# Backward chain of a memory-augmented attention kernel: gradient stores from the last step of a block on, two loads and one gather moved with them

## The chip, the cores and the metric

The kernel runs on one core of one Trainium2 chip. The metric is the device time of one execution in microseconds (us), and the time of a kernel is the median of its runs. Before the change it is 2886.74 us, the median of three runs between 2880.99 and 2886.81 us.

## What is computed

The reference is the forward pass and all gradients of `x + A(layernorm(x)) + B(layernorm(x))`. B is a two-layer network with a squared ReLU. A is a recurrent attention: the 2048 rows are cut into 64 segments of 32 rows, and each segment attends to itself and to 8 memory rows that the segment before it produced.

```python
for s in range(n_seg):                       # 64 segments of 32 rows
    h = concat([mem, xs], axis=1)            # 8 memory rows + 32 rows
    q, k, v = h @ Wq, h @ Wk, h @ Wv         # 512 -> 32 heads of 128
    p = softmax(where(mask, q @ k.T * scale, -1e9))
    o = (p @ v) @ Wo
    mem = o[:, :M]                           # carried to the next segment
    outs.append(o[:, M:])
```

The gradients run through the segments in the reverse order, because the gradient of `mem` is carried from segment s to segment s - 1. That part is the backward chain.

## The kernel before

Activations and weights are bf16, sums are float32 in PSUM. The kernel has stages that follow each other: the norm and network B, the forward chain, a stage for the memory rows of all blocks at once (line 992 on), the backward chain (lines 1158 to 1498), and the products that make the weight gradients (line 1501 on).

The backward chain takes one step for each of the 64 segments. Four steps make a block, so there are 16 blocks. The text numbers steps 0 to 3 in the order in which they run within a block, and blocks 0 to 15 in the order in which they run; the program's own index `b` counts down, and the last block that runs is the one with `b == 0`. A step computes the gradient of the attention output (`o0mm`, `o1mm`, line 374), turns it (`o0fl`, `o1fl`), forms the score gradients (`s0`, `d10` to `d40`, which write the tile `gS`), and from them the gradients of value, key and query: TensorE makes them in the PSUM tiles `b_pp` (`vp`, `kp`, `qp`, lines 1389, 1391 and 623), and ACT or DVE evict them (`vea`, `kea0`, `qeb1` and so on) into three tiles `gv`, `gk`, `gq` (the dictionary `G4`, line 1189). These hold the gradients of all four steps of a block in one buffer each, of 8 KB a partition. From them the gathers `vg`, `kg`, `qg` (line 492) sum the gradient of the input into `ps_gR`, and `ra` to `Hb` close the chain to the next step.

The order of all work is written out by hand. `B_ORDER` (line 1158) has one string for each of the four steps, and `play` (line 652) goes through the names: each name is a small function that emits instructions. A plain name is an operation of a step; with "L." ahead it belongs to a block. The number of plus signs says by how much the operation is ahead of its place. `L.x++` in the string of step 3 belongs to the block whose step 3 runs, `L.x+` to the block before. The engines take their own instructions in this order, each waiting on semaphores only for what it needs. An engine whose next instruction has nothing to wait for runs ahead of the others, so a name's place in the string fixes the order on its engine, not a moment.

The names that the change touches:

- `vo0`, `vo1`, `ko0`, `ko1`, `qo0`, `qo1` (line 1243): the six stores of a block's `gv`, `gk`, `gq` to the DRAM tensor `S_GB`, 512 KB each, issued on the SP queue. A value store covers half of the groups; a key or query store covers half of the heads of each group. The next block's evictions overwrite the same tiles, so they wait for the stores.
- `ldk0`, `ldk1` (line 1342): two loads of 128 KB on the SP queue into `b_kNL`, the key rows of the memory positions. They are read by `qp0` and `qp1` (line 623). The tile has one buffer, so they wait for the last `qp` of the block before.
- `L.G0` (line 1256): the first eight of the matmuls that gather the gradient of the memory rows ("left" rows) of a block into `ps_RL`. It reads `b_gvL`, which `vla` writes. In step 3 it stands after `tu1`.

Names that stay but stand around them on the SP queue: `vtr` (line 1346, a transposing load into `b_vl` for a coming step), `L.ldt` (line 632, a transposing load), `L.qtr` (line 1279, a transposing DMA from `b_gqL` to `gNat`), `L.lq` (line 1221, the load into `b_gqL` for the next gathers), `L.qst` (line 1288, a store of `gNat`), `L.sx` (line 1291, a store of `b_XT`). The GpSimd queue (POOL) carries the other loads: `ldp`, `ldq`, `ldn` for each step (`b_P`, `b_qN`, `b_kN`, lines 1332, 1339, 1340) and `L.ldv`, `L.ldk` for each block (lines 1305 to 1310). `pb` (line 1337) copies `b_P` on POOL.

Of the kernel before, what the change touches and what calls it, by code (L numbers as in the profile page):

```python
# [26 lines left out]
def kernel(  # L27
# [35 lines left out]
    L = M + SEG  # L63
# [146 lines left out]
    with sb("p1b", 2) as p1b, sb("p1", 1) as p1:  # L210
# [90 lines left out]
        for rb in range(NRB):  # L301
# [38 lines left out]
            xb = xq[rb]  # L340
# [307 lines left out]
    def on_engines(act, vec):  # L648

        return dict([(n, acp) for n in act.split()] + [(n, vcp) for n in vec.split()])  # L650
# [50 lines left out]
    with psum("fr", 4) as fr, psum("fpp", 1) as fpp, \  # L701
# [259 lines left out]
        with tc.manual_schedule():  # L961
            steps, lefts = [], {-1: left_projections(1, {})}
            for s in range(NSEG):
                steps.append(fwd(s))
            for b in range(NB):
                lefts[b] = left(b)
            steps[0]["ld0"]()
            for p in range(2):
                for g in range(HG):
                    x = slice(g * KH + 4 * p, g * KH + 4 * p + 4)  # L970
                    dma(Wo[:, x], A_Wo.rearrange("h e d -> e h d")[:, x])

            early = []
            after = {"ob0": 2, "ob1": 2, "L.S1": 2, "L.ex0": 2, "L.ex1": 2, "L.tu1": 4, "L.ob1": 2, "L.G1": 1, "L.G0": 1}
            after_o = {"L.ra": 6, "L.tb": 5, "L.xt": 5}

            def done(k):
                if k == "L.lq":  # L980
                    early.append(xlp.tile([P, KH, HG, NL], BF16, name="l_vT0", tag="XL1"))
                    turned_rows(early[0][:], SEQ[0], 2)
                for q, m in ((TURNS, after.get(k, 0)), (TURNS_O, after_o.get(k, 0))):
                    for i in range(m):
                        ps = fr.tile([P, 8 * P], BF16, name="ps_wt", tag="r")
                        turn_weight(ps, *q.pop(0), acp if k in ("L.S1", "L.ex0", "L.ex1") else (acp, vcp)[i % 2])
            for n in range(-1, NB + 4):
                play(F_ORDER, n, steps, lefts, lambda s: s, lambda b: b, done)
# [5 lines left out]
    with sb("la", 2) as la, sb("ls", 2) as ls, sb("lo", 1) as lo_, sb("wg", 2) as wg, psum("lpp", 1) as lpp, psum("lr", 4) as lr:  # L994
# [161 lines left out]


    B_ORDER = (
# [17 lines left out]
        "ta++++ rb++++ Ha++++ tb++++ Hb++++",  # L1176
# [5 lines left out]
        "ta++++ L.qst+ kla1++++ tb++++ L.H0++ Ha++++ Hb++++")  # L1182
    ENGS = on_engines(
        "L.ra0 kea0 keb0 keb1 kla0 kla1 o0ev o1ev qea0 qea1 qeb0 ra vea veb vla vlb",
        "kea1 klb0 klb1 o0te o1te qeb1")
    with sb("bq", 1) as bq, sb("bt", 1) as bt, sb("bs", 2) as bs, sb("be", 1) as be, psum("bpp", 1) as bpp, psum("br", 4) as br:
# [30 lines left out]
        def left(b):  # L1217
            B_ = block(b)
            ps, st, o = {}, {}, {}
# [19 lines left out]
            for t, n in enumerate("qkv"):  # L1239
                for x in range(2):  # L1240
                    def so(n=n, t=t, gs=slice(2 * x, 2 * x + 2) if n == "v" else slice(0, HG),
                           ks=slice(0, KH) if n == "v" else HALF[x]):
                        dma(S_GB[b, t][:, gs, ks], G4[n][:, gs, ks].rearrange("p g k j r -> p g k (j r)"))
                    o["%so%d" % (n, x)] = so

            jobs = [(turned_heads(Wqkv[t]), src[n], k) for t, n in ((2, "v"), (1, "k"), (0, "q")) for k in range(KH)]
            for i in range(4):
# [213 lines left out]
        with tc.manual_schedule():  # L1461
# [3 lines left out]
            for b in range(NB):  # L1465
                lefts[b] = left(b)
# [35 lines left out]
    with sb("p5a", 1) as p5a, sb("p5h", 1) as p5h, sb("p5", 2) as p5, sb("p5g", 1) as p5g, \  # L1502
# [118 lines left out]
        for i, (t, g) in enumerate(COLS):  # L1621
# [14 lines left out]
            for x, js in enumerate(jobs[k:k + each] for k in range(0, len(jobs), each)):  # L1636
                if x in ((), (), (2, 6), (2, 6))[i] if i < 4 else x == 4:
                    b = todo.pop(0)
# [48 lines left out]
```

## Time and profile before

| | |
|---|---|
| Median of three runs | 2886.74 us |
| The profiled execution's own time | 2877.56 us |
| Its span (first to last instruction) | 2875.8 us |
| Mean granted TensorE clock | 0.976 of full speed |
| TensorE matmuls busy | 2677.1 us (93% of the span) |
| Backward chain, first step's start to last step's end | about 1336 to 2290 us |

The profile is of one execution. Times in it count from the start of the span. A row of the windows view gives a stretch, its length, the busy time of each engine in it with the number of instructions in brackets, the granted TensorE clock, the busy share of the 16 DMA engines and the rate in GB/s. A row of the waits view says who waited for whom, how long in total, how often, and the longest wait. In a timeline row the last bracket is the idle time of the engine just before, and what ended it; "issue" stands there when the profile shows nothing that the engine waited for.

### The profile page before, as it was taken

What the parts mean: (1) busy time and instruction counts of PE and PEld (TensorE: products, weight loads), DVE (VectorE), ACT (ScalarE), POOL (GpSimd) and SP (SyncE); (2) the same over time, 40 slices, a digit from 0 to 9 for tenths busy, and PEclk for the clock granted to TensorE, in tenths of its full rate; (3) what the DMA queues carried; (4) which work ended last, traced back from release to release, by engine and by line L of the source; (5) the groups of instructions that cost most, each with busy time, mean ns of one, the idle gap of its engine ahead of it and who ended that gap; (6) DMA issues with size and microseconds to landing.
All of it is one profiled execution on the core that took longest, in us unless ns stands there. A gap on an engine that the chain in (4) does not pass through costs nothing.

```text
span 2875.8 us, 116940 instructions
## 1 busy us (share of the span) xinstructions
PE 2677.1 (93%) x52315; PEld 1444.3 (50%) x52405; DVE 1277.7 (44%) x3755; ACT 1001.4 (35%) x2330; POOL 664.9 (23%) x1289
## 2 busy tenths in 40 slices
PE   7998999999999996988988999989998899999999
PEld 3444555555555555465544455545454444444444
DVE  4534656666666654444444455544454401100000
ACT  2324444444444545232433333333333311111111
POOL 1010000000000001223433333433334334322221
PEclk9999999999999998999999999999999999999999
DMA  9765589899899998996677766886787799999992
GB/s 254 262 207 170 157 203 222 206 218 222 206 215 225 207 219 204 286 243 181 163 171 210 182 172 176 182 219 167 173 179 186 223 271 246 212 211 212 218 218 65
DMA packets 839066, 586.77 MB, mean 204 GB/s; under 512 B 638001, under 2 KB 727618, under 8 KB 835234
## 3 DMA queue, kind: packets, MB, share of 16 engines
q1 hardware_dynamic: 796034, 450.52, 69.3%
q0 software_dynamic: 42384, 128.63, 14.9%
q8 instruction: 411, 6.73, 1.0%
q14 instruction: 93, 0.76, 0.1%
q10 hardware_dynamic: 144, 0.13, 0.0%
HBM read 184.95 MB, written 248.79 MB: 151 GB/s over the span
## 4 chain that ended last, share of the span: by engine, by line
PE 82%; DMA 6%; issue 4%; DVE 4%; SPq 2%; ACT 1%; POOL 1%; ACTq 0%; DVEq 0%; POOLq 0%
PE ps_gw L1645 19%; PE ps_proj L374 15%; PE ps_gR L492 11%; PE ps_R L492 4%; PE ps_tr L167 3%; PE ps_L L374 3%; PE b_pp L623 3%; DMA b_qN<-S_A 2%; PE ps_RL L1256 2%; PE f_pp L623 2%; PE ps_sc L464 2%; PE ps_h L310 2%; PE ps_B L345 2%; PE ps_gxb L354 2%; PE f_T L528 2%
## 5 line engine op out<-in xcount | busy, mean ns | idle before, releaser
L1645 PE MATMUL ps_gw<-gn,HNc 128*128 128x512 bf16 x1884 | 414.6, 379 | 1.9
L1645 PEld LDWEIGHTS <-HNc 128*128 128x128 bf16 x1920 | 187.9, 98 | 223.8
L419 ACT CAST f_N<-ps_proj 128x512 bf16<-128x512 f32 x320 | 184.0, 581 | 195.5 <-PE ps_proj L374 185.7
L1579 ACT CAST wt<-ps_gw 128x512 bf16<-128x512 f32 x128 | 73.4, 589 | 440.6 <-PE ps_gw L1645 387.1
L374 PEld LDWEIGHTS <-X 128*32 128x32 bf16 x5760 | 144.3, 96 | 137.5 <-DVE X L537 21.2
L884 POOL COPY kM<-f_kT 128x256 bf16<-128x256 bf16 x64 | 25.8, 403 | 750.0 <-DVE f_kT L422 562.6
L1562 DVE TENSOR_TENSOR gx<-ps_rows,gb 128x512 f32<-128x512 f32 x16 | 11.1, 692 | 396.9 <-PE ps_rows L1560 396.9
L492 PE MATMUL ps_gR<-Wv,gv 128*32 128x512 bf16 x2048 | 144.9, 404 | 4.9 <-issue 4.7
L492 PE MATMUL ps_gR<-Wk,gk 128*32 128x512 bf16 (+1 forms) x2048 | 140.9, 387 | 8.0 <-issue 6.0
L1645 PE MATMUL ps_gw<-GOc,gn 128*128 128x512 bf16 x626 | 139.2, 380 | 2.2 <-DMA GOc<-in_grad_out_dram 1.3
L492 PE MATMUL ps_R<-Wo,OT 128*32 128x256 bf16 x4096 | 129.3, 275 | 8.1 <-DMA Wo<-in_A_Wo_dram 3.8
L419 ACT CAST gON<-ps_proj 128x512 bf16<-128x512 f32 x128 | 75.0, 586 | 161.9 <-PE ps_proj L374 161.9
L374 PE MATMUL ps_proj<-Wo,GT 128*32 128x512 bf16 x2048 | 124.6, 384 | 6.6 <-DVE GT L1301 5.0
L492 PE MATMUL ps_gR<-Wq,gq 128*32 128x512 bf16 (+1 forms) x2048 | 126.3, 356 | 4.4 <-issue 4.4
L374 PE MATMUL ps_proj<-Wq,X 128*32 128x512 bf16 x1920 | 127.8, 380 | 1.2 <-issue 1.1
L1580 POOL DMA_DIRECT2D out_dram<-wt x120 | 65.0, 543 | 265.4 <-ACT wt L1579 239.3
L374 PE MATMUL ps_proj<-Wk,X 128*32 128x512 bf16 x1920 | 124.8, 382 | 1.7 <-issue 1.1
L419 ACT CAST gk<-b_pp 128x256 bf16<-128x256 f32 x192 | 69.2, 379 | 159.0 <-PE b_pp L623 96.6
L374 PE MATMUL ps_proj<-Wv,X 128*32 128x512 bf16 x1920 | 121.5, 378 | 0.0
L1332 POOL DMA_DIRECT2D b_P<-S_A x63 | 33.9, 537 | 370.3 <-DVE gST L482 120.1
L1337 POOL COPY PD<-b_P 32x320 bf16<-32x320 bf16 x256 | 115.5, 451 | 10.0 <-PE ps_tr L167 1.3
L492 PEld LDWEIGHTS <-OT 128*32 128x32 bf16 x4096 | 104.5, 97 | 16.5 <-issue 10.6
(291 smaller groups left out, 5276.6 us busy)
## 6 DMA issues: line engine op xcount, KB each, us to landing
S_A<-f_N SPq DMA_DIRECT2D x64, 512.0 KB
out_dram<-wt POOLq DMA_DIRECT2D x134, 128.0 KB, 5.2
S_A<-f_N SPq DMA_DIRECT2D x64, 256.0 KB
S_GB<-gv SPq DMA_DIRECT2D x32, 512.0 KB
S_GB<-gk SPq DMA_DIRECT2D x32, 512.0 KB
S_GB<-gq SPq DMA_DIRECT2D x32, 512.0 KB
b_kN<-S_A POOLq DMA_DIRECT2D x63, 256.0 KB, 4.3
b_qN<-S_A POOLq DMA_DIRECT2D x63, 256.0 KB, 4.0
```

Of the source, the lines that this page charges most:

```text
L167: nc.tensor.transpose(ps_ap, in_ap, ident[base:base + k, base:base + k])
L310: nc.tensor.matmul(ps[:], lhsT=W1[:, dc, fc * P:(fc + 1) * P], rhs=HT[:, dc, :], start=(dc == 0), stop=(dc == DC - 1))
L345: nc.tensor.matmul(psB[:], lhsT=aT[:, fc, rc * P:(rc + 1) * P], rhs=W2[:, fc, :], start=(fc == 0), stop=(fc == FC - 1))
L354: nc.tensor.matmul(psG[:], lhsT=gh1T[:, fc, rc * P:(rc + 1) * P], rhs=W1T[:, fc, :], start=(fc == 0), stop=(fc == FC - 1))
L374: nc.tensor.matmul(o, lhsT=hT[:, dc, :], rhs=x, start=(dc == 0), stop=(dc == DC - 1), tile_position=(0, 32 * g))
L419: nc.scalar.copy(out, in_)
L492: nc.tensor.matmul(R[32 * g:32 * g + 32, 0:(cs.stop - cs.start) * P].rearrange("p (a b) -> p a b", b=P), lhsT=XT(k, g), rhs=x[:, cs, :], s ...
L623: nc.tensor.matmul(o, lhsT=N_[32 * g:32 * g + m, kk * P:(kk + 1) * P], rhs=X(kk)[32 * g:32 * g + m], start=(i == 0), stop=(i == len(jobs) ...
L1337: nc.gpsimd.tensor_copy(PD[32 * g:32 * g + 32, g], C["P"][32 * g:32 * g + 32, :, KW - L:KW])
L1579: nc.scalar.copy(wt[:], ps[:])
L1580: eng(dst, wt[:])
L1645: nc.tensor.matmul(ps[:], lhsT=l(rc), rhs=r(rc), start=(n == 0), stop=(n == RC_ALL - 1))
```

## The change

All edits are in `B_ORDER` and in one line that names the stores.

```diff
     B_ORDER = (
-        "L.vo0+ o0mm++++ o1mm++++ L.vo1+ o0ev++++ pb+++ xa+++ L.xt ldk0+++ o1ev++++ o0fl++++ xb+++ L.ra0+ vp0++++ "
-        "o0te++++ L.G2+ ldk1+++ vea++++ s0++++ ...
+        "L.vo0+ o0mm++++ o1mm++++ L.vo1+ L.Qo1+ o0ev++++ pb+++ xa+++ L.xt o1ev++++ o0fl++++ xb+++ L.ra0+ vp0++++ "
+        "o0te++++ L.G2+ vea++++ s0++++ ...
...
-        "vlb++++ d40++++ d11++++ vg0++++ kp0++++ L.tb+ kla0++++ tu0++++ d21++++ qp0++++ vg1++++ d31++++ keb0++++ "
-        "d41++++ kea0++++ kg0++++ kp1++++ L.qtr+ qeb0++++ tu1++++ L.G0++ klb0++++ qp1++++ L.ldv++ L.ta+ qea0++++ "
-        "qg0++++ qeb1++++ kea1++++ keb1++++ qea1++++ kg1++++ L.lq++ klb1++++ qg1++++ L.I0++ ra++++ L.ldk++ rb++++ "
-        "ta++++ L.qst+ kla1++++ tb++++ L.H0++ Ha++++ Hb++++")
+        "vlb++++ d40++++ d11++++ vg0++++ L.G0++ kp0++++ L.Vo0++ L.Vo1++ L.tb+ kla0++++ tu0++++ d21++++ qp0++++ vg1++++ d31++++ keb0++++ "
+        "d41++++ kea0++++ kg0++++ kp1++++ L.qtr+ qeb0++++ tu1++++ klb0++++ qp1++++ L.ldv++ L.ta+ qea0++++ "
+        "qg0++++ qeb1++++ kea1++++ L.Ko0++ keb1++++ qea1++++ kg1++++ L.lq++ klb1++++ qg1++++ L.I0++ ra++++ L.ldk++ L.Ko1++ rb++++ "
+        "ta++++ L.qst+ ldk0++++ ldk1++++ L.Qo0++ kla1++++ tb++++ L.H0++ Ha++++ Hb++++")
...
-                    o["%so%d" % (n, x)] = so
+                    o["%so%d" % (n.upper() if b > 0 else n, x)] = so
```

For every block but the last, the stores have capital names and stand from step 3 of their own block on. For the last block they keep the small names and the old places. As built, the SP queue of one block boundary takes its DMAs in these orders:

```
before: vtr, ldt, qtr, lq, qst, vo0, vo1, ldk0, ldk1, ko0, qo0, qo1, sx, vtr, ko1, vtr
after:  vtr, ldt, Vo0, Vo1, qtr, Ko0, lq, Ko1, qst, ldk0, ldk1, Qo0, Qo1, sx, vtr, vtr
```

In the built program `Vo0` waits for the second eviction of `gv` in step 3 (ACT), `lq` waits for the landing of `qtr`'s transposes, whose source it overwrites, and `ldk0` waits for the last `qp1` of the block. TensorE, ACT, DVE and POOL execute the same instructions as before; on TensorE only `G0` stands elsewhere, ahead of `kp0` in step 3 of all 16 blocks.

2 rows, old and new, of the table B_ORDER are left out of this document.

## The prediction

> **What bounds the kernel now.** I began with the page: how much TensorE idles at all.
>
> ```profile
> span 2875.8 us, 116940 instructions
> PE 2677.1 (93%) x52315; PEld 1444.3 (50%) x52405; DVE 1277.7 (44%) x3755; ACT 1001.4 (35%) x2330; POOL 664.9 (23%) x1289
> q8 instruction: 411, 6.73, 1.0%
> ```
>
> TensorE is busy 93% of the span, so time is won only where it idles or runs at a lower clock. To find where, I cut the chain at the first `ps_proj` matmul of each step and asked for the windows of 15 blocks (1 to 15): all steps 1, then 2, then 3 (each the step ahead of a boundary), then 0. Of each answer this is the sum row; one quick step of either kind stands ahead of it for the last two.
>
> ```profile
> sum 196.30, PE 194.00 PEld 107.77 DVE 118.76 ACT 80.29 POOL 74.42; mean PE 12.93 PEld 7.18 DVE 7.92 ACT 5.35 POOL 4.96
> sum 196.00, PE 189.30 PEld 105.21 DVE 95.03 ACT 84.39 POOL 65.47; mean PE 12.62 PEld 7.01 DVE 6.34 ACT 5.63 POOL 4.37
> 1855.80:1869.50 13.70, 13.57 (x365) 7.48 (x368) 7.50 (x24) 5.50 (x15) 7.98 (x16) 1.00 0.81 179
> sum 227.70, PE 209.59 PEld 114.00 DVE 118.62 ACT 82.45 POOL 126.75; mean PE 13.97 PEld 7.60 DVE 7.91 ACT 5.50 POOL 8.45
> 1756.40:1770.70 14.30, 13.24 (x368) 7.33 (x360) 6.94 (x24) 6.03 (x16) 4.21 (x8) 1.00 0.82 216
> sum 273.10, PE 220.83 PEld 113.57 DVE 103.39 ACT 90.75 POOL 72.58; mean PE 14.72 PEld 7.57 DVE 6.89 ACT 6.05 POOL 4.84
> ```
>
> Steps 1 and 2 take 13.1 us and are full. Step 3 takes 227.7 / 15 = 15.2 us and step 0 takes 18.2 us, though quick ones take 13.70 and 14.30. So there is an excess of 273.1 - 15 x 14.3 = 58.6 us in the steps 0 and of 227.7 - 15 x 13.7 = 22.2 us in the steps 3. That is all this change can win. Who TensorE waits for in the chain, by the waits view:
>
> ```profile
> PE b_pp L623 <- issue: 28.3, 19, 4.7
> PE b_pp L623 <- DMA b_qN<-S_A: 15.4, 9, 5.6
> PE ps_gR L492 <- issue: 15.1, 12, 4.0
> PE b_pp L623 <- DVE gS L582: 7.2, 10, 1.0
> PE ps_gR L492 <- DVE gk L422: 1.5, 2, 1.2
> ACT gk L419 <- DMA S_GB<-gk: 15.1, 6, 3.3
> SPq L1221 <- DMA gNat<-b_gqL: 44.6, 15, 4.0
> ```
>
> The largest entries have no releaser ("issue"). I read them as code that arrives late: the page's instruction queue brings 6.73 MB in 411 packets, about 104,800 matmuls and weight loads / 411 = 255 instructions each, over the DMA engines that the stores use. The second entry is a load that lands late. So both are DMA; the DMA share around one boundary (step 3 from 1678.5, step 0 from 1693.6, step 1 from 1712.7) shows when:
>
> ```profile
> 1684.00:1687.00 3.00, 2.35 (x90) 1.45 (x94) 2.38 (x8) 1.22 (x5) 1.44 (x4) 1.00 0.43 87
> 1687.00:1690.00 3.00, 3.00 (x106) 1.54 (x102) 1.00 (x4) 0.67 (x3) 3.00 (x7) 1.00 0.76 217
> 1690.00:1699.00 9.00, 8.81 (x188) 5.08 (x178) 4.30 (x16) 4.09 (x10) 3.15 (x7) 1.00 0.99 329
> 1699.00:1702.00 3.00, 1.61 (x72) 0.85 (x73) 1.52 (x5) 0.37 (x1) 0.54 (x1) 1.00 1.08 382
> 1702.00:1707.00 5.00, 3.60 (x40) 1.22 (x39) 0.57 (x2) 1.04 (x4) 0.00 (x0) 0.57 1.10 270
> ```
>
> The engines are full from 1690 to 1707, 17 us, of which 13.4 lie in step 0. TensorE starves from 1699 on, and then its granted clock falls to 0.57.
>
> The Trainium skill (Runtime: NRT & Kernel Launch, Instruction fetch mechanics) has code arrive in blocks of 256 instructions, and the crossing into the next "mostly hidden". The block size agrees; by the hiding, the two issue rows (43.4 us) would be no DMA matter, and rival 3 below would be the likeliest. Their place in the full stretches speaks against it.
>
> **The change part by part.** First the SP queue at that boundary, as it ran before:
>
> ```profile
> 1681.27 1.47 SPq L1279 DMA_TRANSPOSE gNat<-b_gqL  x1
> 1686.59 0.33 SPq L1221 DMA_DIRECT2D b_gqL<-S_GQL  x1
> 1686.97 0.43 SPq L1288 DMA_DIRECT2D S_GL<-gNat  x1
> 1687.44 1.79 SPq L1243 DMA_DIRECT2D S_GB<-gv  x2
> 1689.33 2.36 SPq L1342 DMA_DIRECT2D b_kNL<-S_NL  x2
> 1691.79 1.25 SPq L1243 DMA_DIRECT2D S_GB<-gk  x1
> 1693.08 1.53 SPq L1243 DMA_DIRECT2D S_GB<-gq  x2
> ...
> 1701.35 1.19 SPq L1243 DMA_DIRECT2D S_GB<-gk  x1
> ```
>
> The stores named for step 0 are issued in step 3 already, because SP runs ahead. So the change moves less than its names say. *The gather.* In step 3 TensorE ends `vg0`, waits for `gS`, and then runs `kp0`; `G0` takes 0.61 us later on:
>
> ```profile
> 1684.60 0.20 PE L623 MATMUL b_pp<-gS,b_qN 32*128 32x40 bf16 x4 [0.65 <-DVE gS L582]
> 1687.99 0.61 PE L1256 MATMUL ps_RL<-Wv,b_gvL 128*32 128x512 bf16 x8
> 1683.38 0.27 ACT L419 CAST b_gvL<-b_pp 128x128 bf16<-128x128 f32 x1
> ```
>
> `G0` needs `b_gvL`, whose last eviction ends at 1683.65, before the gap opens at 1683.95. So eight matmuls of 0.61 us fill a gap of 0.65 us, and leave their old place without a wait there, since `qp1` behind them was ready. All gS waits are 7.2 us in 10 cases: the term is -7.2 us, between 0 (if code arrives late at that place) and 16 x 0.61 = -9.8.
>
> *The value stores* go ahead of `qtr`: ready at 1683.65, they start 1687.44 - 1683.65 = 3.8 us earlier, into engines with room: 3 x (1 - 0.43) + 3 x (1 - 0.76) = 2.4 us of full work. With as many bytes in all, the full stretch would end 2.4 us earlier: 11.0 instead of 13.4 us in step 0, -18%. If the step-0 excess shrinks in proportion: -58.6 x 0.18 = -10.5 us. In step 3 the full stretch grows by the same 2.4 us to what is there: 3.6 us from 1690 on and 5.5 from 1678.5 to 1684 with transposes, a quarter more; of its excess without the gS waits, 22.2 - 7.2 = 15.0, that is +4.0. Net -6.5 us. Bounds: the whole step-0 excess (-58.6) and the step-3 excess doubled (+15).
>
> *The second key store* comes from 1701.35 ahead of the query stores. The next block's key evictions wait 15.1 us for it on ACT; behind ACT stands the key gather, and TensorE's own wait for `gk` is 1.5 us. I take -1.5 (0 to -15.1).
>
> *What it costs on SP.* `lq` may start only when `qtr` has landed, 1686.59 - 1681.27 = 5.3 us after `qtr` began. Now `qtr` begins after the value stores' 1.79 us of issue, at 1685.4, so `lq` starts at 1690.7, or at 1693.6 if the 1 MB ahead holds it for 1 MB / 329-382 GB/s = 2.9 us. SP works in order: behind `lq` wait `Ko1`, `qst`, both `b_kNL` loads, both query stores, `sx` and the next `vtr`. With the issue times above (0.33 + 1.25 + 0.43, then half of 2.36) the first `b_kNL` load has been issued at 1693.9 to 1696.8 instead of 1690.5. Who waits for it is `qp0` of step 0, 7.3 us into that step in block 11, which starts at 1992.20:
>
> ```profile
> 1999.47 0.20 PE L623 MATMUL b_pp<-gST,b_kNL 32*128 32x32 bf16 x4 [0.66 <-issue]
> 1692.74 7.36 DMA b_qN<-S_A
> ```
>
> The need is at 1693.6 + 7.3 = 1700.9. No row has the landing of a `b_kNL` load. The nearest is `b_qN`'s, 7.36 us in the same crowd, twice the bytes, which makes 1701.3 to 1704.2: 0.4 to 3.3 us late. With half of that delay nothing is late. Bounds 0 and 15 x 3.3 = +50; I take +2, because the value stores ahead are gone earlier and the nine `b_qN` waits already push `qp0` back. The query stores move later too, towards the evictions that overwrite `gq`; the same stall would cover both. With POOL's loads unchanged in order, the sum is -7.2 - 6.5 - 1.5 + 2 = -13.2 us: 2877.56 - 13.2 = 2864.4 for the profiled execution. The median of the runs stands 9.18 above that execution, so 2873.5 for the median.
>
> The clock is in the excess already (clock 0.57 above follows 1.61 us busy in 3.00). The Trainium skill (TensorE: Matmul & The Clock Gate, The HAM clock gate) lowers the clock only after an idle window of some 3.4 us; here it fell after shorter waits, so the trace differs, and a short stall saved counts for more than by the page.
>
> **The rivals.** *1. The crowd thins out for good*, and step 0 comes near its floor. For it: the blocks whose value stores already began early. In four stretches (a step 3 and the step 0 behind it; the first and the last are shown, then the sum of all four) they began 4.4, 6.8, 5.6 and 5.0 us into step 3, against 1687.44 - 1678.5 = 8.9 at the boundary above:
>
> ```profile
> 1382.60:1412.60 30.00, 26.62 (x725) 14.71 (x728) 13.56 (x42) 11.53 (x31) 12.67 (x24) 1.00 0.79 228
> 1974.00:2006.50 32.50, 28.96 (x729) 15.46 (x732) 14.95 (x47) 11.53 (x31) 13.11 (x26) 0.95 0.82 225
> sum 127.20, PE 112.68 PEld 60.54 DVE 58.65 ACT 46.12 POOL 51.98; mean PE 28.17 PEld 15.14 DVE 14.66 ACT 11.53 POOL 12.99
> 1386.98 1.55 SPq L1243 DMA_DIRECT2D S_GB<-gv  x2
> 1979.03 0.96 SPq L1243 DMA_DIRECT2D S_GB<-gv  x2
> ```
>
> They take 127.2 / 4 = 31.8 us, the other eleven (500.8 - 127.2) / 11 = 34.0. Eleven times 2.2 and the gather make -31 us: 2855.7. Against it: there `qtr` had gone first, and the other stores were early too.
>
> *2. SP stalls at `lq`* (the slower side): value stores hold `qtr`, `lq` holds `b_kNL`, and `qp0` waits. It decides once the load lands over 7.3 us into step 0. Price 2 us in each of 15 boundaries, +30, less the gather's 7.2 and the key store's 1.5: +21, 2908. For it: SP waits here 3.0 us a block even now (44.6 in 15). Against it: the late `b_qN` (9 waits) already holds the matmuls ahead of `qp0`.
>
> *3. The waits only move*: what step 0 wins comes back in step 3, where code is now late among `kp` and `qp`; the gather's gain is left, and 2 us of it lost: 2881.5, at the edge of what can be told. For it: the bytes are the same, SP had run ahead anyway.
>
> **How the numbers follow.** Chances: forecast 0.35 (its own range 2865 to 2882), rival 1 0.17, rival 2 0.30, rival 3 0.18. A measurement here tells about 0.2%, 5.8 us, from no change. Faster: 0.33 + 0.17 + 0.02 = 0.52; same: 0.02 + 0.12 = 0.14; slower: 0.30 + 0.04 = 0.34. The range 2852 to 2908 leaves out half of rival 2 and a quarter of rival 1, 0.19.
>
> **What would show it.** The gather: the gS wait of 7.2 us gone from TensorE's waits. The stores: mean step 0 near 17.5 us, step 3 near 15.0, the ACT wait for `S_GB` gone. Rival 1: step 0 under 16.5. Rival 2: `lq` issued over 12 us into step 3, TensorE waiting for `b_kNL`, or ACT for the `gq` stores. Rival 3: issue waits in step 3 up by what they lose in step 0. A step 3 above 17 us would prove the forecast wrong.

## The result and the profile after

| | before | after |
|---|---|---|
| Median of 20 runs each | 2888.54 us | 2875.47 us |
| Lowest to highest run | 2864.89 to 2906.11 us | 2860.19 to 2895.03 us |
| Ratio, 95% interval | 1 | 0.9958 [0.9940, 0.9976] |
| Profiled execution | 2877.56 us | 2877.35 us |

The change is faster by 13.1 us (6.9 to 17.3 us by the interval). Here and below, the ratios leave out the few executions that are over 1.5% slower than the fastest of their kernel, and the medians in us do not. A single execution lies up to 24 us from the median, so one profile cannot show such a difference in its span:

```profile
span 2875.6 us, 116922 instructions
PE 2672.8 (93%) x52315; PEld 1447.4 (50%) x52405; DVE 1277.0 (44%) x3755; ACT 1001.7 (35%) x2330; POOL 665.8 (23%) x1289
```

The span is 0.2 us shorter than before's. The difference lies inside: the backward chain (first step's start to last step's start) takes 932.7 us instead of 939.1, but in this execution it began 11.9 us later, behind stages that the change does not touch, and what follows its last step's start took 5.7 us less. So I compare stretches of the chain. These are the windows of the same 15 blocks as in the prediction, all steps 1, then 2, 3 and 0; of each answer the sum row.

```profile
sum 196.90, PE 194.65 PEld 108.41 DVE 118.70 ACT 80.20 POOL 73.98; mean PE 12.98 PEld 7.23 DVE 7.91 ACT 5.35 POOL 4.93
sum 195.10, PE 187.71 PEld 104.45 DVE 94.94 ACT 84.41 POOL 66.32; mean PE 12.51 PEld 6.96 DVE 6.33 ACT 5.63 POOL 4.42
sum 233.00, PE 209.69 PEld 116.27 DVE 117.66 ACT 82.47 POOL 125.89; mean PE 13.98 PEld 7.75 DVE 7.84 ACT 5.50 POOL 8.39
sum 260.40, PE 217.20 PEld 113.30 DVE 103.67 ACT 90.91 POOL 73.38; mean PE 14.48 PEld 7.55 DVE 6.91 ACT 6.06 POOL 4.89
```

Steps 1 and 2 stay within 1 us of before (196.3 and 196.0). The steps 0 lose 12.7 us (from 273.1), the steps 3 take 5.3 us more (from 227.7). How far such sums can be trusted shows in the run without the exception for the last block, further down: up to its last step it has the order of the change, and its execution gave 255.3 us for the steps 0 and 227.6 us for the steps 3. So two executions of the same order lie some 5 us apart in each sum, and the loss in the steps 0 is clear, the 5.3 us in the steps 3 are not. Who waits in the chain now (the waits view; who for whom, total, times, longest):

```profile
PE b_pp L623 <- issue: 28.5, 23, 3.2
PE ps_gR L492 <- issue: 19.8, 17, 3.8
PE b_pp L623 <- DMA b_qN<-S_A: 8.5, 4, 3.8
PE b_pp L623 <- DMA b_kNL<-S_NL: 2.3, 4, 1.1
PE b_pp L623 <- DVE gS L582: 1.9, 3, 1.3
ACT gq L419 <- DMA S_GB<-gq: 4.7, 5, 1.1
SPq L1221 <- DMA gNat<-b_gqL: 61.9, 15, 5.2
```

Against before, TensorE's wait for `gS` falls from 7.2 to 1.9 us, and that for `b_qN` from 15.4 to 8.5. ACT's wait for the key stores (15.1) is gone, and one for the query stores (4.7) is there. The unnamed issue waits do not fall: 48.3 us in these two rows, 43.4 before. They change their place: summed over the 15 boundaries, all issue waits of TensorE in the steps 0 fall from 34.4 to 26.9 us, and those in the steps 3 rise from 8.9 to 19.5. SP waits longer at `lq`, 61.9 instead of 44.6 us. One boundary of after in windows (step 3 begins at 1697.1, step 0 at 1712.5, step 1 at 1728.5), and then SP's timeline there:

```profile
1703.00:1706.00 3.00, 2.97 (x112) 1.48 (x100) 1.96 (x6) 1.41 (x5) 2.22 (x5) 1.00 0.96 339
1706.00:1709.00 3.00, 2.05 (x84) 1.02 (x68) 0.98 (x3) 0.70 (x2) 2.92 (x7) 1.00 1.26 81
1709.00:1712.50 3.50, 3.48 (x66) 2.14 (x70) 0.98 (x4) 0.70 (x2) 2.19 (x5) 1.00 1.06 387
1712.50:1715.50 3.00, 3.00 (x57) 1.61 (x53) 1.63 (x7) 1.63 (x4) 0.00 (x0) 1.00 1.05 385
1715.50:1718.50 3.00, 2.96 (x108) 1.93 (x104) 2.38 (x8) 1.81 (x6) 0.00 (x0) 1.00 1.06 380
1718.50:1721.50 3.00, 1.04 (x48) 0.51 (x40) 0.67 (x3) 0.00 (x0) 0.54 (x1) 1.00 1.39 333
1721.50:1724.50 3.00, 3.00 (x80) 1.28 (x80) 1.00 (x3) 1.41 (x5) 0.53 (x1) 1.00 0.49 111
```

```profile
1701.66 1.41 SPq L1243 DMA_DIRECT2D S_GB<-gv  x2
1703.11 1.58 SPq L1279 DMA_TRANSPOSE gNat<-b_gqL  x1
1704.81 0.57 SPq L1243 DMA_DIRECT2D S_GB<-gk  x1
1710.22 0.33 SPq L1221 DMA_DIRECT2D b_gqL<-S_GQL  x1
1710.66 0.54 SPq L1243 DMA_DIRECT2D S_GB<-gk  x1
...
1713.80 1.60 SPq L1243 DMA_DIRECT2D S_GB<-gq  x2
```

The value stores go out 4.6 us into step 3 and fill the engines (0.96, 339 GB/s). Behind them the transposes of `qtr` occupy them (1.26) while few bytes move (81 GB/s). `lq` waits for those transposes and leaves 13.1 us into step 3; the second key store and the query stores stand behind it. The crowd ends at about 1721.5, 9 us into step 0, where before it ended at 1707, 13.4 us in. It costs TensorE 1.96 us of one window, and in these windows the clock stays at 1.00.

### The profile page after: what moved, and what is told of

Read it like the earlier page. It is cut to its first block, busy times and chain, and to the rows that moved or that the text cites. A ratio compares the mean times of both kernels' runs of the same rounds, so it can differ in the third digit from the quotient of the medians.

```text
span 2875.6 us, 116922 instructions
## 1 busy us (share of the span) xinstructions
PE 2672.8 (93%) x52315; PEld 1447.4 (50%) x52405; DVE 1277.0 (44%) x3755; ACT 1001.7 (35%) x2330; POOL 665.8 (23%) x1289
## 3 DMA queue, kind: packets, MB, share of 16 engines
q0 software_dynamic: 42384, 128.63, 15.2%
## 4 chain that ended last, share of the span: by engine, by line
PE 84%; DMA 6%; issue 4%; DVE 4%; ACT 1%; SPq 1%; POOL 0%; ACTq 0%; DVEq 0%; POOLq 0%
PE ps_gw L1645 19%; PE ps_proj L374 16%; PE ps_gR L492 11%; PE ps_R L492 5%; PE ps_tr L167 3%; PE ps_L L374 3%; PE b_pp L623 3%; PE ps_RL L1256 2%; PE ps_sc L464 2%; PE f_pp L623 2%; PE ps_w L1106 2%; PE ps_h L310 2%; PE ps_B L345 2%; PE ps_gxb L354 2%; PE ps_ga L317 2%
## 5 line engine op out<-in xcount | busy, mean ns | idle before, releaser
L419 ACT CAST f_N<-ps_proj 128x512 bf16<-128x512 f32 x320 | 184.0, 581 | 196.0 <-PE ps_proj L374 189.3
L492 PE MATMUL ps_R<-Wo,OT 128*32 128x256 bf16 x4096 | 131.8, 279 | 11.9 <-issue 6.3
L492 PEld LDWEIGHTS <-OT 128*32 128x32 bf16 x4096 | 105.7, 98 | 21.0 <-issue 14.1
```

The lines of the kernel that those rows point to most:

```text
L419: nc.scalar.copy(out, in_)
L492: nc.tensor.matmul(R[32 * g:32 * g + 32, 0:(cs.stop - cs.start) * P].rearrange("p (a b) -> p a b", b=P), lhsT=XT(k, g), rhs=x[:, cs, :], s ...
```

## The experiments

Every ratio is against the kernel before on the same chip. A profile is one execution: the sums over 15 steps that stand with a run belong to it alone.

**The gather alone** (the kernel before, `G0` moved):

```diff
-vg0++++ kp0++++ ... tu1++++ L.G0++ klb0++++
+vg0++++ L.G0++ kp0++++ ... tu1++++ klb0++++
```

> The kernel before with the left gather G0 alone ahead of kp0 in step 3; the stores and loads stay. Theory (the gather fills the wait for gS): TensorE's wait for gS in the chain falls from 7.2 us in 10 cases to under 2.5 us, the sum of the 15 steps 3 falls by some 5 us from 227.7, the steps 0 stay at 273 within what one execution differs from the next (15 us); time 0.995 to 1.000 of before. Rival (the whole gain of the change is in the stores): the gS wait goes, but the code that arrives late takes its place: steps 3 at 227 or above, time 1.000.

Measured: 1.0008 [0.998, 1.0037] (2889.95 us). The steps 3 take 225.4 us against 227.7 in before, the steps 0 282.2 against 273.1. The next block's key evictions wait longer for the key stores (the waits view; ACT's row was 15.1 before):

```profile
PE b_pp L623 <- DVE gS L582: 3.8, 3, 1.7
ACT gk L419 <- DMA S_GB<-gk: 26.8, 9, 4.4
DVE gk L422 <- DMA S_GB<-gk: 10.1, 4, 3.9
```

Of TensorE's 3.8 us for `gS` only 0.3 lie in a step 3, so the wait there goes away as expected, but no time is won by it that these runs can tell; the interval allows at most 5.8 us. In this execution the issue waits in the steps 3 are 14.1 us instead of 8.9.

**The stores without the gather** (the change, `G0` back behind `tu1`):

```diff
-vg0++++ L.G0++ kp0++++ ... tu1++++ klb0++++
+vg0++++ kp0++++ ... tu1++++ L.G0++ klb0++++
```

> The changed kernel with the left gather back in its old place: stores and loads moved alone. Theory: the gS wait stays near 7 us; the sum of the steps 0 falls from 273 to about 262, the sum of the steps 3 rises by 4 to 232; ACT's wait of 15.1 us for the key stores is gone; time 0.996 to 0.999 of before. Rival (the stores only move the waits): steps 0 and 3 together stay at 500.8 within 5 us and the time is 1.000. Rival (the SP queue stalls at lq and costs time): together over 510 us, TensorE waits for b_kNL over 10 us.

Measured: 0.9972 [0.9938, 1.0006] (2876.81 us), steps 3 238.9, steps 0 248.8. The wait for `gS` came to 4.1 us in 6 cases, not near 7, though `G0` stands in its old place. The ratio cannot be told from the whole change, nor quite from no change. The stores' order carries the gain as far as it can be seen; the run with the value stores alone, below, shows it more clearly.

**`qtr` ahead of the value stores** (the change, SP's old order of these two):

```diff
-kp0++++ L.Vo0++ L.Vo1++ ... kp1++++ L.qtr+ qeb0++++
+kp0++++ L.qtr+ L.Vo0++ L.Vo1++ ... kp1++++ qeb0++++
```

> The changed kernel with the transposes of b_gqL (qtr) ahead of the value stores on SP again, so that lq is not held by 1 MB of stores. Theory (lq costs SP time behind the value stores): SP's wait at lq for the transposes, 61.9 us in 15 cases in the changed kernel, falls to 45 or less; the second key store, the b_kNL loads and the query stores start 2 to 4 us earlier; TensorE's wait for b_kNL (2.3 us) and ACT's for the query stores (4.7 us) go; time 0.3% under the changed kernel, 0.992 to 0.996 of before. Rival (nothing that TensorE waits for hangs on lq): the SP order changes as said, and the time is that of the changed kernel, 0.996 of before; with the crowd packed into a shorter time the code waits in steps 3 and 0 may even grow.

Measured: 1.0004 [0.9972, 1.0036] (2884.83 us). SP's wait at `lq` is gone, and so is the gain. Steps 3 and 0, then two rows of the waits:

```profile
sum 239.40, PE 213.78 PEld 117.11 DVE 118.59 ACT 82.46 POOL 126.45; mean PE 14.25 PEld 7.81 DVE 7.91 ACT 5.50 POOL 8.43
sum 257.00, PE 217.24 PEld 113.77 DVE 102.26 ACT 90.45 POOL 70.07; mean PE 14.48 PEld 7.58 DVE 6.82 ACT 6.03 POOL 4.67
```

```profile
PE b_pp L623 <- DMA b_qN<-S_A: 16.8, 10, 4.8
SPq L1221 <- DMA gNat<-b_gqL: 6.9, 4, 4.0
```

So the wait that the prediction priced at +2 us does not cost here: without it the ratio is 0.46% higher, though the ends of the two intervals (0.9972 and 0.9976) still touch. With `lq` free, the second key store leaves on the mean 4.8 instead of 2.5 us ahead of step 0, and the two query stores 1.3 and 0.5 us ahead of it instead of 0.4 and 1.3 us behind: the stores stand closer together. `b_qN`, loaded beside them on POOL's queue, is late again, 16.8 us in all. The two sums of this execution, 496.4 us together, are hardly above the 493.4 us of the change, so the loss rests on the ratio alone.

**No stores in blocks 0 to 14** (the kernel before; the stores of these blocks are left out, and the products at the end read the stored block in their place):

```diff
-dma(S_GB[b, t][:, gs, ks], ...)
+if b == 0: dma(S_GB[b, t][:, gs, ks], ...)
...
-S_GB[4 * q + x, t][:, g]
+S_GB[0, t][:, g]
```

> The kernel before without the stores of gv, gk and gq of 15 of the 16 blocks; the weight gradients are then formed from the stored block alone, read as often, so that the stage behind the chain has the same work. Theory (the excess of steps 0 and 3 is the stores' traffic, through code and loads that arrive late): the steps 0 come to 14.3 to 15 us each (sum 215 to 225 instead of 273.1), the steps 3 to 14.2 (213 instead of 227.7), TensorE's issue waits fall from 51 us to under 10, its wait for b_qN from 15.4 to under 2; time 55 to 70 us under before, 0.976 to 0.981. Rival (code arrives late whatever the stores do, or the POOL loads make the crowd): issue waits stay over 25 us, the steps 0 over 250, and the time falls by less than 30 us.

Measured: 0.9822 [0.9772, 0.9873] (2834.02 us). Steps 3 and 0, then TensorE's waits:

```profile
sum 228.20, PE 210.21 PEld 113.95 DVE 118.55 ACT 82.46 POOL 126.97; mean PE 14.01 PEld 7.60 DVE 7.90 ACT 5.50 POOL 8.46
sum 202.40, PE 197.90 PEld 109.36 DVE 103.58 ACT 90.45 POOL 66.70; mean PE 13.19 PEld 7.29 DVE 6.91 ACT 6.03 POOL 4.45
```

```profile
PE b_pp L623 <- issue: 13.5, 15, 3.6
PE b_pp L623 <- DVE gS L582: 8.4, 12, 0.9
PE ps_gR L492 <- issue: 4.6, 6, 1.7
```

The steps 0 lose 70.7 us and come to 13.5 us each. So the floor is lower than the 14.3 us that the prediction took, and all of the excess there belongs to the stores. The steps 3 do not change (228.2 against 227.7): their excess is not the stores'. The issue waits fall from 43.4 to 18.1 us, and no wait for `b_qN` over 0.2 us is left.

**No stores, and the gather** (the kernel of the run before, `G0` moved as in the first run):

> The kernel before without the stores of gv, gk and gq of 15 blocks (the weight gradients are formed from the stored block alone) and with the left gather ahead of kp0. Theory (the gather fills a gap of 0.65 us that is real, and the crowd of the full kernel hides it): the gS wait falls from 8.4 us to under 2, the sum of the steps 3 from 228.3 by 6 to 222, the time to 2827, 0.9795 of before against 0.9822 without the gather. Rival (the gap comes back at the next wait of TensorE on DVE or ACT, or code is late instead): the gS wait goes, but the steps 3 stay at 226 to 230, and the time stays at 0.982.

Measured: 0.9753 [0.9701, 0.9805] (2814.04 us). The steps 3 fall to 216.5 us, from 228.2, and TensorE's wait for `gS` from 8.4 to 0.9:

```profile
sum 216.50, PE 204.73 PEld 115.81 DVE 118.26 ACT 82.40 POOL 127.76; mean PE 13.65 PEld 7.72 DVE 7.88 ACT 5.49 POOL 8.52
PE b_pp L623 <- DVE gS L582: 0.9, 3, 0.3
```

With no crowd, the steps 3 are 11.7 us shorter with the gather moved, of which the wait for `gS` is 7.5; the rest is no more than two executions differ by, and the two ratios overlap in their intervals. The issue waits in the steps 3 stay (8.1 without and 8.5 with the move), where beside the stores they rose from 8.9 to 14.1. So it seems that with the crowd late code takes the place of the wait that is saved; these are single executions, and it is not shown.

**The query stores later** (the change, `Qo0` behind `sx` and `Qo1` behind `vtr`, both in step 0):

```diff
-L.vo1+ L.Qo1+ o0ev++++ ... L.sx+ vg0++++ ... vtr++++ L.ko1+ ... ldk1++++ L.Qo0++ kla1++++
+L.vo1+ o0ev++++ ... L.sx+ L.Qo0+ vg0++++ ... vtr++++ L.Qo1+ L.ko1+ ... ldk1++++ kla1++++
```

> The changed kernel with the first query store behind sx and the second behind the transposing load vtr in step 0, so that the last 1 MB of stores is spread further. Theory (the gain of the change is that the stores of a block are spread out, the hold at lq included, and loads and code get through between them): TensorE's wait for b_qN falls from 8.5 us to under 5, its issue waits from 51 to about 45; the price is ACT waiting for the query stores, 4.7 us before, now up to 25 us; time 0.993 to 0.998 of before. Rival (what counts is that the stores are over early in step 0): the steps 0 rise from 260 to 270 or more, and the time is 1.000 or above.

Measured: 0.9922 [0.9887, 0.9957] (2857.43 us), the lowest ratio of all kernels that compute everything, and it beats before. Against the change (0.9940 to 0.9976) the intervals overlap, so that it also beats that one is likely, not shown. Steps 3 and 0, and the waits:

```profile
sum 232.90, PE 209.84 PEld 116.55 DVE 120.09 ACT 82.46 POOL 131.00; mean PE 13.99 PEld 7.77 DVE 8.01 ACT 5.50 POOL 8.73
sum 243.20, PE 209.84 PEld 113.72 DVE 102.65 ACT 91.11 POOL 70.96; mean PE 13.99 PEld 7.58 DVE 6.84 ACT 6.07 POOL 4.73
```

```profile
PE b_pp L623 <- DMA b_qN<-S_A: 4.3, 7, 1.2
ACT gq L419 <- DMA S_GB<-gq: 23.9, 12, 3.4
```

The steps 0 lose another 17.2 us against the change, though ACT now waits 23.9 us for the late query stores. What such a wait of ACT costs, if anything, is less than what is won.

**`qtr` first and the query stores late** (the two edits above together):

> The kernel with late query stores (ratio 0.9922) with `qtr` put back ahead of the value stores, as in the run with `qtr` first (ratio 1.0004). The wait of SP at `lq` then falls from 59.0 us to under 10 us again, but the query stores are spaced by their places in the order and not by that wait. Theory (the wait at `lq` was worth keeping only because it held the query stores back): with them held back by hand, its loss costs little, the ratio is 0.991 to 0.995, TensorE's waits for b_qN stay under 9 us and the steps 0 near 243 us. Rival (what cost the run with `qtr` first its gain is the order itself: the transposes of `qtr` lie among the value stores and slow what runs beside them in step 3): the ratio is 0.997 to 1.001, the steps 3 take over 238 us as they did there (239.1) and the b_qN waits are near 16 us.

Measured: 0.9930 [0.9898, 0.9961] (2867.11 us); the steps 3 take 230.6 and the steps 0 253.9 us.

```profile
PE b_pp L623 <- DMA b_qN<-S_A: 11.7, 9, 2.3
SPq L1221 <- DMA gNat<-b_gqL: 6.6, 3, 4.5
```

The wait at `lq` is gone here too, but with the query stores held back by hand the gain is there. Its interval and that of `qtr` first (0.9972 to 1.0036) do not meet. So `qtr` ahead of the value stores is not by itself what cost that run its gain: where the query stores stand decides it. In the change it is the wait at `lq` that holds them back, and with them the second key store and the loads of `b_kNL`, which were not tried by themselves. The `b_qN` wait and the steps 0 came out higher than the theory had them (11.7 us for under 9, 253.9 for 243), in an execution 9.4 us above its median.

**The value stores alone early** (the kernel before):

```diff
-vg0++++ kp0++++ L.tb+
+vg0++++ kp0++++ L.Vo0++ L.Vo1++ L.tb+
...
-o["%so%d" % (n, x)] = so
+o["%so%d" % (n.upper() if b > 0 and n == "v" else n, x)] = so
```

> The kernel before with the two value stores alone moved to step 3 (behind kp0); key stores, query stores, b_kNL loads and the gather stay where they were. Theory (value stores into free DMA time, and the hold at lq delaying what follows, are the gain): the steps 0 fall from 273 to 255 to 262, b_qN's wait from 15.4 to about 9, and ACT's wait for the second key store stays at 10 us or more; time 0.996 to 0.999 of before. Rival (the second key store, which no longer comes at 7 us into step 0, is the gain): steps 0 at 268 or above, time 1.000.

Measured: 0.9936 [0.9901, 0.9971] (2864.18 us), steps 3 242.9, steps 0 245.2. As far as these runs can tell, it gets as much as the whole change, so none of the other moves is shown to win anything on top. ACT waits 20.6 us for the key stores, more than the 15.1 before, and the kernel is faster all the same.

**The key store alone early** (the kernel before):

```diff
-L.ko0+ d30++++ ... vtr++++ L.ko1+ kg0++++
+L.ko0+ L.ko1+ d30++++ ... vtr++++ kg0++++
```

> The kernel before with the second key store alone moved, from behind the transposing load in step 0 to directly behind the first key store; four stores then leave in one burst. Theory (spreading is the gain): ACT's wait for the key stores (15.1 us) goes, but the burst makes code or b_qN later, steps 0 at 270 or above; time 0.999 to 1.005. Rival (the second key store's place was a part of the gain, as the prediction had it with 1.5 us): steps 0 under 268, time 0.997 or less.

Measured: 0.9988 [0.9955, 1.0021] (2888.08 us), steps 3 224.1, steps 0 277.2; ACT still waits 13.7 us for the key stores and TensorE 15.8 for `b_qN`. This part has no gain that can be told. It draws the bunch closer: the second key store leaves on the mean 1.5 us ahead of step 0, where before it left 6.4 us behind its start.

**`b_qN` loaded earlier** (the change, the load ahead of `pb` in POOL's order of step 0):

```diff
-o0ev++++ pb+++ ... ldp++++ ldq+++ veb++++
+o0ev++++ ldq+++ pb+++ ... ldp++++ veb++++
```

> The changed kernel with step 0's load of b_qN ahead of the copies of b_P and of the loads of b_kN and b_P on the POOL queue; it starts 3 us earlier. Theory (b_qN is late because it is the last of 0.6 MB of loads in a crowd): TensorE's wait for b_qN goes from 8.5 us to under 2, that for b_kN or b_kNL rises by less than 3 us, the steps 0 fall from 260 by 5 to 10; time 0.991 to 0.995 of before. Rival (code is late there anyway, so that another issue wait takes the place): the b_qN wait goes, the issue waits rise by as much, and the time stays at 0.996.

Measured: 0.9946 [0.9913, 0.9978] (2867.27 us), steps 3 237.4, steps 0 264.3. The wait for `b_qN` is gone; the issue waits of the chain are higher:

```profile
PE b_pp L623 <- issue: 39.8, 25, 4.3
PE ps_gR L492 <- issue: 23.4, 17, 4.4
```

They sum to 63.2 us against 48.3 in the change. In this execution at least as much as is saved on the load is waited for on the issue rows, and the ratio is inside the interval of the change.

**Stores by when their tiles are next written** (the change, `Qo0` in the place of `Ko1`, `Ko1` behind `sx`, `Qo1` behind `vtr`):

```diff
-L.ldk++ L.Ko1++ rb++++ ... ldk1++++ L.Qo0++ kla1++++
+L.ldk++ L.Qo0++ rb++++ ... ldk1++++ kla1++++
...
-L.vo1+ L.Qo1+ o0ev++++ ... L.sx+ vg0++++ ... vtr++++ L.ko1+
+L.vo1+ o0ev++++ ... L.sx+ L.Ko1+ vg0++++ ... vtr++++ L.Qo1+ L.ko1+
```

> The spread of the late-query run with the halves in the order in which the next block overwrites them: both value stores, the first key store, the first query store in step 3, then the second key store behind sx and the second query store behind vtr in step 0. Theory (spreading is the gain, and its price is ACT waiting for query stores that come too late): ACT's wait for the query stores falls from 23.9 us to under 8, that for the key stores stays under 10; the steps 0 stay near 243 or below; time 0.989 to 0.993 of before, not above the late-query run's 0.9922 by more than the interval. Rival (those waits are hidden behind other waits, so only the spread counts): the waits go, the time stays at 0.992.

Measured: 0.9947 [0.9917, 0.9977] (2869.25 us), steps 3 228.4, steps 0 257.9. ACT's wait for the query stores is 28.5 us in 8 cases instead of shorter: the last store, `Qo1`, is a query store again. No gain over the change can be told.

**No exception for the last block** (the change, capital names for all blocks):

```diff
-n.upper() if b > 0 else n
+n.upper()
```

> The changed kernel without the exception of the last block: its stores, too, stand from its own step 3 on. Theory (the exception is of no weight, because no next block crowds there): time that of the changed kernel, 0.994 to 0.998 of before, the stretch from the last step's start to the end of the span at 594 to 600 us. Rival (the stores of the last block hold up the end of the chain or the first loads of the next stage): that stretch over 603 us, time 0.998 or more.

Measured: 1.0017 [0.9987, 1.0047] (2896.32 us). The rest of the chain has the order of the change (steps 3 227.6, steps 0 255.3, against 233.0 and 260.4 in the change's own execution), but from the last step's start to the span's end it takes 619.6 us (2894.0 - 2274.4) instead of 594.4 (2875.6 - 2281.2). SP's timeline and longest wait there:

```profile
2280.19 5.63 SPq L1279 DMA_TRANSPOSE gNat<-b_gqL  x1
2303.74 0.33 SPq L1221 DMA_DIRECT2D b_gqL<-S_GQL  x1
2305.74 4.67 SPq L1243 DMA_DIRECT2D S_GB<-gq  x2
```

```profile
SPq L1221 <- DMA gNat<-b_gqL: 73.8, 15, 16.5
```

In the last block the loads of the next stage run beside the stores (the DMA share is 1.05 from 2290 to 2305 us), and `lq` leaves 29.3 us into the step (2303.74 - 2274.4), after a wait of up to 16.5 us, with the second key store and the query stores behind it. The first `ps_gw` matmul of the next stage begins 56.1 us after the last step's start, in the change 30.9. So in the last block the early stores, with this wait, cost 25 us where TensorE has little left to run meanwhile, and without the exception the change gains nothing.

## Why the prediction came out, and where its steps failed

The sum was right: 2873.5 us against 2875.47, and -13.2 against -13.1 us. That it fits to 0.1 us is luck: the interval of the measurement runs from 6.9 to 17.3 us, and the terms were not all right; errors of both signs cancelled. The profiled execution shows -7.4 us in the stretches (-12.7 + 5.3), the other execution of the same order (that of the run without the exception) -17.9 (-17.8 - 0.1).

*The value stores, -10.5 in step 0 and +4.0 in step 3.* The first half held roughly: 12.7 us left the steps 0, and 17.8 in the other execution of this order, of the 70.7 that the run without stores puts down to them. That is 18% and 25%; 18% was forecast. The mean step 0 is 17.4 us, 17.5 was forecast. (The excess itself was taken too low, 58.6, because the quick step still held some of it. And the stores were ready at 1683.49, when ACT's eviction of `gv` ended (1682.90 + 0.59 in its timeline), not at 1683.65, which is that of `b_gvL`; this changes little.) The second half was mis-sized: without the gather the stores alone brought 11.2 us to the steps 3 (238.9 - 227.7), and the value stores alone 15.2 (242.9 - 227.7). With the gather the steps 3 were to lose 3.2 us; they took 5.3 more in the one execution of this order and 0.1 less in the other. The step that failed is "of its excess without the gS waits": without stores it stays, 14.3 of 15.0 us (228.2 - 205.5 - 8.4), so it was not the stores' and no base for their price.

*The gather, -7.2.* The wait for `gS` went away, as forecast, from 7.2 to 1.9 us (0.6 of it in the steps 3). But by the runs of the gather alone (1.0008) the time did not follow, and with the stores moved the two ratios (0.9972 without it, 0.9958 with it) differ by less than their intervals. The prediction gave 0 as the bound "if code arrives late at that place". What failed is the step that counts a filled wait as time won. The runs fit that bound: without the crowd the gain is there (216.5 against 228.2, one execution each), and with it the issue waits in the steps 3 grow. That late code is what takes the wait's place was not tried by itself. With both terms, the steps 3 were forecast at 15.0 us and came out at 15.5, and at 15.2 in the other execution.

*The second key store, -1.5.* No run shows it; moved alone it gave 0.9988 [0.9955, 1.0021], which is too wide for 1.5 us. Its bound of -15.1, all of ACT's wait, has little for it: ACT's waits for stores are 20.6 us with the value stores alone and 23.9 us with late query stores, both faster kernels than before.

*SP at `lq`, +2.* The timing was right: `lq` leaves 13.1 us into step 3 at the boundary shown, and TensorE waits for `b_kNL`, 2.3 us in 4 cases, near the +2. But the sign of what the wait at `lq` is worth was wrong. The prediction counted who waits behind `lq`, and not that what waits there are stores that are better late. Taking the wait away costs the gain (1.0004), and holding the query stores back by hand brings it back (0.9930). By these two runs the wait is worth more than the +2 us were to cost. I read this as the stores standing less densely; that simply fewer bytes fall beside the load of `b_qN` would look the same, and no run separates the two.

*The rivals.* The first, a thin crowd, did not come: step 0 stayed above 16.5 us. With late query stores it comes there, 16.2 us (243.2 / 15), and the gain, 22.4 us against before on the same chip (2879.87 - 2857.43), lies between the forecast and the 31 us of this rival. The second had its mark, `lq` later than 12 us, in most blocks, but not its price, except in the last block, which the change leaves out. The third is partly true. Its mark came: the issue waits in the steps 0 fell by 7.5 us, and those in the steps 3 rose by 10.6. And an earlier `b_qN` turned its wait into issue waits. But the steps 0 lost more than the steps 3 took back, which this rival did not allow.

## What to carry to other kernels

Stores that nobody waits for soon are better spread over the time until their tile is written again than sent as early as they are ready, as far as these runs show; a queue's wait that looks like a stall may be what spreads them, so it is tried before it is removed. A wait that vanishes from one engine is a gain only if nothing else ends just behind it: run it once with the suspected crowd taken away. A sum over one execution is compared with that of a second execution of the same order before a few us are read from it. The last turn of a loop, where the next stage waits for the stores, wants its own order.

## What the runs showed of the hardware

TensorE's issue waits stand at fixed distances of instructions. Three windows of after, each from the end of one long issue wait to the end of the next, with the number of matmuls and weight loads in brackets:

```profile
1414.90:1422.70 7.80, 3.97 (x128) 2.15 (x127) 2.76 (x9) 2.16 (x7) 0.54 (x1) 1.00 0.87 174
1422.70:1469.30 46.60, 42.52 (x1147) 22.86 (x1147) 22.96 (x69) 17.32 (x47) 20.97 (x41) 0.95 0.66 131
1709.00:1721.25 12.25, 10.26 (x253) 5.99 (x254) 5.67 (x20) 4.15 (x10) 2.73 (x6) 1.00 1.15 378
```

128 + 127 = 255, 1147 + 1147 = 2294 and 253 + 254 = 507: near 1, 9 and 2 times 256. Counted with TensorE's semaphore instructions, which the windows leave out, all 24 issue waits over 0.85 us in the chain of after lie within 2 instructions of a multiple of 256 from the first. That fits code arriving in blocks of 256 instructions and waited for at the border. The Trainium skill (Runtime: NRT & Kernel Launch, Instruction fetch mechanics) has the same block and calls the crossing "mostly hidden". By count the trace agrees: the first and the last of the 24 waits are 158 such blocks apart. But 43.4 us were not hidden beside the stores, and 18.1 us without them.

The crowd also costs clock: of the 15 steps 0, 11 ran below the full clock before (0.82 to 0.92), 8 in the change and none without the stores. Over the whole profiled execution the granted clock averages 0.985 without the stores and 0.976 before.
